# Idle products cut from 512 to 256 columns, and one ones-column memset left out

## The chip, the cores and the metric

The kernel runs on one core of one Trainium2 chip. The metric is the device time of one launch in microseconds (us), taken as the median of several runs. A core has five engines with queues of their own: PE (matrix products; its weight loads are shown as PEld), DVE (vector), ACT (activations), POOL and SP (here a DMA queue only). Each engine takes its instructions in order; they meet through semaphores.

## What is computed

Four batches, eight heads, 768 tokens, head size 64. A small 8 x 8 matrix per head is normalised five times by rows and columns (Sinkhorn) and mixes the eight blocks of 96 tokens of K and of V. Each block of Q attends to the block of the same index. The result, 768 x 512 per batch, goes through a gated MLP with a product over the tokens. Cut to what matters:

```python
for _ in range(5):
    P = np.exp(P - np.max(P, axis=-1, keepdims=True))
    P = P / (np.sum(P, axis=-1, keepdims=True) + 1e-09)
    P = P / (np.sum(P, axis=-2, keepdims=True) + 1e-09)
k_sorted = einsum('bhij,bhjcd->bhicd', P, k_blocks)
v_sorted = einsum('bhij,bhjcd->bhicd', P, v_blocks)
attn = softmax(scale * q_blocks @ k_sorted.T)        # per block
x = (attn @ v_sorted)                                # 4 x 768 x 512
h = np.maximum(x @ w_in, 0.0)                        # 512 -> 1024
u, v = h[..., :512], h[..., 512:]
v_n = (v - mu) / np.sqrt(var + 1e-06)
v_s = einsum('ts,bsd->btd', w_spatial, v_n) + b_spatial[None, :, None]
out = (u * v_s) @ w_out
```

## The kernel before

The order of the work is written out by hand: the string ORDER (L18 to L53) is a list of units such as `AT:0:3:2:0`, each of which calls the function of that name (`u_AT`) with its arguments, and the instructions go to each engine's queue in that order. A unit's first argument is often a PSUM tile: 0 to 3 are pairs of banks, 10 to 17 are single banks, so that tile 0 is banks 10 and 11. The four batches overlap: while batch 1 is in its MLP, attention of batch 2 and 3 is already under way.

The parts that the change touches or that stand around it:

- **Idle products** (`u_DM`, L232 to L235): products of a zeroed tile `warm` with itself into a PSUM tile whose content nobody reads. The arguments are the PSUM tile, the number and the columns of each. 12 stand at the start, ahead of the transposes of Q. Then `DM:12:5:512` and `DM:12:4:512` stand between two groups of transposes of Q (L324), and `DM:10:2:512` stands behind the products that spread P over the partitions (`u_PR`, L265), ahead of V's first mixing products (L393), which need pd. pd is written by DVE (`u_P0`, L279) from the spread P. P comes from DVE's Sinkhorn steps (`u_SK`, L247 to L260).
- **V with its ones column.** For batches 1, 2 and 3, V's mixed blocks are built in the tile `vm` (`u_VM`, L420 to L428), 66 columns per head: 64 of V and two of ones. DMAs from SP's queue copy whole rows, all 66 columns, from `vm` to `vb[b % 2]` (`u_VC`, L433): four DMAs for blocks 0 to 3, four for blocks 4 to 7. The ones column makes the attention product (`u_AT`, L498) give the row sums too, in its 65th column.
- **Three memsets** on POOL write the ones (`u_IV`, L230): `IV:0` into `vb[0]` and `IV:2` into `vm` at the start, and `IV:1` into `vb[1]`, far later: in ORDER it stands in batch 3's attention (L38), behind the issue of V's first four copies of batch 3 (`VC:3:0:4`) and ahead of the second four. Batch 1, which uses `vb[1]` too, ran by then on what the copies had brought.
- **The gate.** For batch 1's four quarters of 128 features (`mc`), the product over tokens (`u_SP`, L619) goes into a PSUM tile, DVE adds the bias (L625) and writes a tile `z`, POOL multiplies z by u (`u_GT`, L636) into `gt`, and the output products (`u_OP`, L645) read gt. There are three z buffers. The gate products of batch 1 stand on POOL directly behind `IV:1`: `GT:P:1:3`, `GT:P:1:1`, `GT:P:1:0`, `GT:P:1:2`. The fourth z (`SP:0:1:2`) takes the buffer that the first gate product frees.
- **What follows it on PE:** `SP:0:1:2`, then scores of batch 3 (`SC:1:3:2:0`, `SC:2:3:2:1`, L452, each with exponentials on ACT, L457), the v half of the MLP's first layer for batch 2 (`VP:16:A:2:5`, L564) and attention of batch 3 (`AT:0:3:2:0`, L498), which writes the same PSUM tile 0 that the addition of `SP:0:1:2` reads.

The last stretch of the order, behind `IF`, runs after a branch on a flag that says that all sums were in range.

Of the kernel before, what the change touches and what calls it, by code (L numbers as in the profile page):

```python
# [16 lines left out]

ORDER = """  # L18
S0 CO DM:10:5:512 IV:0 LH:A:0 TB SK:0 DM:10:3:512 L:q:0:4:8 BH ID SK:1 SK:2 IV:2 QC:A:0 DM:10:4:512 QC:A:1 SK:3 MA
L:v:0:0:8 MC SK:4 QQ:0:A:0:0 DM:12:5:512 DM:12:4:512 L:k:0:0:8 QT:12:D:0:3 PR:13 L:v:1:0:8 MB DM:10:2:512 P0:0:2  # L20
P0:2:4 P0:4:6 P0:6:8 VT:2:A:0:0 PC:A VT:3:D:0:1 QT:12:A:0:2 VB:10:D:0:0 PD:1:0:4 VB:11:A:0:1 VT:2:D:0:3 L:k:1:0:8
VT:3:A:0:2 KT:1:D:0:2 KT:0:A:0:0 KT:2:D:0:1 PD:1:4:8 KT:3:A:0:3 L:q:1:0:8 SC:1:0:2:1 VB:10:D:0:2 VB:11:D:0:3 L:wv L:wu
SC:2:0:3:0 SC:3:0:3:1 L:wsb AT:1:0:2:1 SC:0:0:1:0 L:wsa AT:2:0:3:0 SC:1:0:0:0 AT:3:0:3:1 VM:0:A:1:1 AT:2:0:1:0
# [11 lines left out]
VP:10:D:1:3 SC:1:2:3:0 SC:3:2:1:0 ST:1:0 GT:P:0:1 ST:1:4 QP:A:3:2 ST:1:3 UP:2:A:1:0:1 OP:0:0:2:2 ST:1:5 AT:1:2:2:1  # L35
OE:A:0:2 AT:3:2:3:0 OP:2:0:0:2 LN:1:0:6 LA:1:0 LA:1:5 LA:1:1 QP:A:3:3 OE:A:0:0 OP:0:0:4:2 OE:A:0:4 LA:1:4 LA:1:3
VM:1:A:3:3 VM:3:A:3:1 QP:A:3:0 LA:1:2 SP:2:1:0 XD:2:1 QX:3:0:4 VM:0:A:3:2 AT:1:2:0:0 SP:3:1:1 L:k:3:0:8 VM:2:D:3:0
AT:0:2:1:0 SP:1:1:3 OS:0:2:0:2 UP:3:A:1:1:1 VC:3:0:4 AT:2:2:2:0 KT:0:A:3:0 IV:1 KT:1:D:3:1 XD:2:0 GT:P:1:3 KT:3:D:3:2  # L38
GT:P:1:1 KT:2:A:3:3 SP:0:1:2 SC:1:3:2:0 SC:2:3:2:1 VP:16:A:2:5 AT:0:3:2:0 VP:17:D:2:3 SC:1:3:3:0 SC:2:3:0:1 OS:0:4:0:2
ST:2:3 ST:2:5 SC:0:3:1:1 VP:16:D:2:4 VC:3:4:8:0:4 AT:1:3:3:0 VP:17:A:2:0 UP:2:A:2:1:1 AT:0:3:2:1 VP:16:D:2:2 ST:2:2  # L40
SC:1:3:0:0 ST:2:0 GT:P:1:0 SC:2:3:1:0 SC:0:3:3:1 ST:2:4 VP:17:A:2:1 UP:1:A:2:1:0 ST:2:1 UP:2:A:2:0:0 GT:P:1:2 LN:2:0:6
# [795 lines left out]
```

## Time and profile before

| what | value |
|---|---|
| time, median of 3 runs | 155.23 us (154.25 to 155.38) |
| profiled execution | 155.29 us, of which span 153.5 us |
| busy PE, PEld | 142.8 us (93%), 94.5 us (62%) |
| busy DVE, ACT, POOL | 114.7 us (75%), 85.0 us (55%), 42.5 us (28%) |
| chain that ended last, by engine | PE 77%, DVE 11%, issue 3%, ACT 2%, DMA 2%, POOL 1% |
| memsets of L230 on POOL | 3, of 0.18 to 0.21 us, the last at 91.45 us |
| idle products of L235 | 23 of 512 columns |

The span runs from the first to the last instruction of the core; the time of a run has a little around it. In a row of the timeline, the first two numbers are the start and the duration in us, counted from the span's start; behind the engine and the line stand the operation, the tile that is written and the tiles that are read, and in brackets the idle time of the engine before it, with what ended it. "issue" there means that the engine waited for nothing that the profile shows. In the chain, each row is a piece of the path that ended last. Ends of products on PE are modelled; their starts are recorded.

### The profile page before, as it was taken

How to read it: one execution, taken by the hardware profiler on the slowest of the kernel's cores; microseconds unless marked ns; L12 is line 12 of the kernel's file. 1: busy time of each engine (PE TensorE's matmuls, PEld its weight loads, DVE VectorE, ACT ScalarE, POOL GpSimd, SP SyncE). 2: the span in 40 equal slices, each digit the busy share in tenths (PEclk: the TensorE clock that was granted, in tenths of full speed). 3: DMA queues.
4: the chain of work that ended last, by engine and by line, in shares of the span. 5: the costliest groups of instructions: out<-in, count | busy, mean ns of one | idle time of the engine just before them, and what ended most of it. 6: DMA issues, size and time to landing. Idle time of an engine off the chain costs nothing.

```text
span 153.5 us, 4093 instructions
## 1 busy us (share of the span) xinstructions
PE 142.8 (93%) x1676; PEld 94.5 (62%) x1676; DVE 114.7 (75%) x264; ACT 85.0 (55%) x122; POOL 42.5 (28%) x47
## 2 busy tenths in 40 slices
PE   6578989989999999999999997999999999999791
PEld 2246867854777666855876674558865556855550
DVE  3788889956797882969964965897927989876632
ACT  4464999875889615978976055786230331520040
POOL 7402994290000004832000019500000800005610
PEclk9999999999999999999999999999999999999999
DMA  4999999999999990899993999000093033039046
GB/s 107 253 204 204 189 198 201 208 219 239 233 258 204 204 158 12 146 149 191 205 168 38 293 208 253 9 0 4 0 263 78 4 137 137 2 134 407 22 178 234
DMA packets 30695, 24.38 MB, mean 159 GB/s; under 512 B 10384, under 2 KB 27792, under 8 KB 30672
## 3 DMA queue, kind: packets, MB, share of 16 engines
q0 software_dynamic: 14432, 12.19, 50.1%
q1 hardware_dynamic: 14864, 9.92, 24.6%
q10 hardware_dynamic: 1376, 1.97, 3.7%
q8 instruction: 14, 0.23, 0.6%
q14 instruction: 9, 0.07, 0.1%
HBM read 24.78 MB, written 6.29 MB: 202 GB/s over the span
## 4 chain that ended last, share of the span: by engine, by line
PE 77%; DVE 11%; issue 3%; ACT 2%; DMA 2%; POOL 1%; SPq 1%; ACTq 0%; DVEq 0%; POOLq 0%
PE ps L564 13%; PE ps L607 13%; PE ps L619 13%; PE ps L645 10%; PE ps L675 5%; PE ps L498 5%; PE ps L452 4%; PE ps L695 4%; PE ps L393 3%; PE ps L420 3%; PE ps L528 2%; DMA vb<-vm 2%; PE ps L324 2%; DVE x_sb L506 2%; PE ps L411 1%
## 5 line engine op out<-in xcount | busy, mean ns | idle before, releaser
L636 POOL TENSOR_TENSOR gt<-z,u_sb 128x768 bf16<-128x768 f32 x9 | 14.6, 1637 | 49.6 <-DVE z L625 26.4
L457 ACT ACTIVATE ex_all<-ps 96x768 bf16<-96x768 f32 x32 | 23.9, 805 | 6.0 <-PE ps L452 5.6
L619 PE MATMUL ps<-wspT,v_sb 128*128 128x384 bf16 x144 | 24.9, 326 | 0.0
L564 PE MATMUL ps<-w_in_sb,xT 128*128 128x512 bf16 x96 | 23.4, 380 | 0.0
L607 PE MATMUL ps<-xT,w_in_sb 128*128 128x384 bf16 x128 | 23.1, 326 | 0.0
L506 DVE TENSOR_TENSOR x_sb<-ps,rec_all 96x512 bf16<-96x512 f32 x32 | 22.0, 687 | 1.1
L625 DVE TENSOR_TENSOR z<-ps,b_bc 128x768 f32<-128x768 f32 x12 | 11.4, 954 | 14.2 <-PE ps L619 12.0
L619 PEld LDWEIGHTS <-v_sb 128*128 128x128 bf16 x144 | 13.7, 98 | 8.7
L127 ACT ACTIVATE v_sb<-ps 128x512 bf16<-128x512 f32 (+1 forms) x15 | 9.9, 657 | 15.9 <-DVE bad L722 8.7
L581 DVE BATCH_NORM_STATS2 stats<-v_sb 128x6 f32<-128x512 bf16 x24 | 16.2, 674 | 1.7 <-ACT v_sb L127 1.5
L607 PEld LDWEIGHTS <-w_in_sb 128*128 128x128 bf16 x128 | 12.1, 98 | 7.9
L645 PE MATMUL ps<-w_out_sb,gt 128*128 128x256 bf16 x144 | 16.9, 273 | 0.0
L121 ACT COPY o_sb<-ps 128x1024 f32<-128x1024 f32 (+1 forms) x10 | 8.8, 883 | 13.9 <-PE ps L695 11.4
L127 ACT ACTIVATE u_sb<-ps 128x768 bf16<-128x768 f32 x12 | 9.7, 810 | 10.3 <-PE ps L607 10.3
L645 PEld LDWEIGHTS <-gt 128*128 128x128 bf16 x144 | 13.9, 98 | 2.1
L564 PEld LDWEIGHTS <-xT 128*128 128x128 bf16 x96 | 8.4, 98 | 8.4
L498 PEld LDWEIGHTS <-ex_all 96*128 96x128 bf16 x256 | 10.7, 97 | 4.5 <-issue 1.6
L498 PE MATMUL ps<-vb,ex_all 96*128 96x65 bf16 x256 | 11.8, 193 | 1.0 <-DVE z L625 0.8
L291 POOL TENSOR_TENSOR pd<-mask,prep_sb 128x512 bf16<-128x512 bf16 x6 | 6.6, 1102 | 13.7 <-ACT prep_sb L121 8.9
L688 POOL TENSOR_TENSOR gt<-z,u_sb 128x512 bf16<-128x512 f32 (+1 forms) x5 | 5.2, 1048 | 18.4 <-DVE z L681 18.4
L121 ACT CAST vm<-ps 128x768 bf16<-128x768 f32 x9 | 7.2, 808 | 4.9 <-PE ps L420 4.7
L452 PE MATMUL ps<-qT,kt_all 64*128 64x96 bf16 x256 | 8.8, 204 | 0.8 <-issue 0.4
(100 smaller groups left out, 205.5 us busy)
## 6 DMA issues: line engine op xcount, KB each, us to landing
out_dram<-o_sb SPq DMA_DIRECT2D x8, 512.0 KB, 3.5
v_in<-in_v_dram POOLq DMA_DIRECT2D x4, 768.0 KB, 13.3
k_in<-in_k_dram POOLq DMA_DIRECT2D x4, 768.0 KB, 10.9
vb<-vm SPq DMA_DIRECT2D x24, 99.0 KB, 3.6
q_in<-in_q_dram POOLq DMA_DIRECT2D x3, 768.0 KB, 25.4
ws_in<-in_moe_w_spatial_dram POOLq DMA_DIRECT2D x2, 576.0 KB, 18.9
w_in_sb<-in_moe_w_in_dram POOLq DMA_DIRECT2D x2, 512.0 KB, 13.2
q<-in_q_dram ACTq DMA_DIRECT2D x1, 768.0 KB, 4.5
```

What stands on the lines that cost most here:

```text
L121: nc.scalar.copy(out=out, in_=in_)
L127: nc.scalar.activation(out=out, in_=in_, func=AF.Relu)
L452: nc.tensor.matmul(t[:, hh, 0:HW].rearrange("p (g x) -> p g x", g=G)[:, :, ii * TB:(ii + 1) * TB], lhsT=kT[rows, i * BLK:i * BLK + 128], r ...
L457: nc.scalar.activation(out=e_tile(b, hp, ih).rearrange("p h (x g) -> p h x g", g=G), in_=t[0:BLK, :, 0:HW].rearrange("p h (g x) -> p h x g ...
L498: nc.tensor.matmul(t[:, hh, ii * VW:ii * VW + D + 1], lhsT=e[:, c:c + 128], rhs=vb[b % 2][:, ih * NI + ii, 2 * hp + hh, 0:D + 1], start=Tr ...
L506: nc.vector.tensor_mul(out=x_sb[:, hp].rearrange("p i (h d) -> p h i d", h=2), in0=tv[:, :, :, 0:D], in1=_raw_ap(rec, 0, [rec.ap[0], [NI, ...
L564: nc.tensor.matmul(t[:, x, :], lhsT=st["xT", b][:, n // 3, kc, (n % 3) * 128:(n % 3 + 1) * 128], rhs=w_in_sb[:, kc, DH:DFF], start=(kc == ...
L581: nc.vector.bn_stats(out=stats, in_=st["v_sb", b, n])
L607: nc.tensor.matmul(t[:, x, 0:HW], lhsT=w_in_sb[:, kc, mc * 128:(mc + 1) * 128], rhs=st["xT", b][:, ih, kc, :], start=(kc == 0), stop=(kc = ...
L619: nc.tensor.matmul(t[:, x, 0:HW], lhsT=st["v_sb", b, n][:, mc * 128:(mc + 1) * 128], rhs=wspT[:, 3 * x:3 * x + 3, n, :], start=(n == 0), s ...
L636: eng.tensor_mul(out=gt, in0=st["z", b, mc], in1=u)
L645: nc.tensor.matmul(t[:, x, c:c + w], lhsT=st["gt", b, mc][:, (n0 + x) * 128:(n0 + x + 1) * 128], rhs=w_out_sb[:, mc, c:c + w], start=(mc = ...
```

## The change

The 11 later idle products of 512 columns become 22 of 256, so that the columns are the same in number. The 12 at the start stay. The memset of the ones columns of `vb[1]` is taken out of the order; the functions stay as they are.

```diff
-L:v:0:0:8 MC SK:4 QQ:0:A:0:0 DM:12:5:512 DM:12:4:512 L:k:0:0:8 QT:12:D:0:3 PR:13 L:v:1:0:8 MB DM:10:2:512 P0:0:2
+L:v:0:0:8 MC SK:4 QQ:0:A:0:0 DM:12:10:256 DM:12:8:256 L:k:0:0:8 QT:12:D:0:3 PR:13 L:v:1:0:8 MB DM:10:4:256 P0:0:2
...
-AT:0:2:1:0 SP:1:1:3 OS:0:2:0:2 UP:3:A:1:1:1 VC:3:0:4 AT:2:2:2:0 KT:0:A:3:0 IV:1 KT:1:D:3:1 XD:2:0 GT:P:1:3 KT:3:D:3:2
+AT:0:2:1:0 SP:1:1:3 OS:0:2:0:2 UP:3:A:1:1:1 VC:3:0:4 AT:2:2:2:0 KT:0:A:3:0 KT:1:D:3:1 XD:2:0 GT:P:1:3 KT:3:D:3:2
```

On the engines' queues: PE has 11 weight loads and 11 products more, in two places (9 pairs become 18, and 2 pairs become 4). POOL has one memset less, with its wait for five DMA semaphores. SP's second four V copies no longer wait for POOL. DVE's and ACT's queues are the same. Each idle product loads its weights anew, before as after.

## The prediction

> **What bounds the kernel now.** I read the page first, then the table of six stretches, then the chain of waits between 82 and 95 us, then PE's list of waits, and last the timeline around both edits.
>
> ```profile
> span 153.5 us, 4093 instructions
> ```
> ```profile
> 85.00:94.30 9.30, 8.47 (x109) 5.41 (x108) 6.58 (x10) 4.24 (x6) 2.85 (x3) 1.00 1.07 273
> 94.30:144.00 49.70, 49.70 (x413) 32.07 (x412) 39.56 (x88) 17.09 (x27) 10.74 (x8) 1.00 0.30 98
> ```
> The columns of the second fence are the stretch, its length, then the busy time of PE, PEld, DVE, ACT and POOL, the granted clock, the DMA share and the GB/s. From 94.30 to 144.00 PE is busy 49.70 of 49.70 us, at a granted clock of 1.00. So a start of PE at 94.3 that comes earlier by x brings the end earlier by x, unless something off PE falls behind. In the stretch before it PE loses 9.30 - 8.47 = 0.83 us, and the waits and the chain say to whom:
>
> ```profile
> PE ps L498 <- DVE z L625: 0.8, 1, 0.8
> ```
> ```profile
> 91.45 0.20 POOL L230 MEMSET vb<- 96x128 bf16 x1 [21.34 <-DMA vb<-vm]
> ```
> ```profile
> 91.45 0.13 POOL vb L230
> 91.58 0.04 issue
> 91.62 1.64 POOL gt L636
> 93.28 0.97 DVE z L625
> 94.25 0.04 issue
> 94.29 0.40 PE ps L498 x8
> ```
> The first fence is PE's list of waits, the second the timeline, the third the chain. The memset that goes is a link of the chain. It waits on POOL for V's first four copies of batch 3, which had therefore landed by about 91.4, it holds back the gate product queued behind it, that product holds a z buffer, the addition that writes z waits for the buffer, and attention (L498) waits for the addition, since both use the same PSUM banks.
>
> **The change part by part. The memset.** It ran 0.20 us, but what counts is when the gate product (L636) could start without it. Its inputs are the z addition at 87.09 and the ReLU that writes u at 88.24:
>
> ```profile
> 75.77 3.49 PE ps L645 x32
> ```
> ```profile
> 87.09 0.94 DVE L625 TENSOR_TENSOR z<-ps,b_bc 128x768 f32<-128x768 f32 x1
> 88.24 0.81 ACT L127 ACTIVATE u_sb<-ps 128x768 bf16<-128x768 f32 x1 [5.09 <-PE ps L607]
> 89.92 2.12 PE L619 MATMUL ps<-wspT,v_sb 128*128 128x384 bf16 x12
> 92.36 1.50 ACT L457 ACTIVATE ex_all<-ps 96x768 bf16<-96x768 f32 x2 [1.54 <-PE ps L452]
> 92.42 1.04 PE L564 MATMUL ps<-w_in_sb,xT 128*128 128x512 bf16 x4
> ...
> 96.11 1.04 PE L564 MATMUL ps<-w_in_sb,xT 128*128 128x512 bf16 x4
> 96.98 0.41 PE L498 MATMUL ps<-vb,ex_all 96*128 96x65 bf16 x8
> ```
> They are ready at 88.03 and 89.05, and the output products that read the last batch's gate tiles ended at 79.26 (first row, of the chain). So the product starts at about 89.1 in place of 91.62 and, at its 1.64 us, ends at about 90.8. The z addition is then no longer held by POOL but by its matmuls, which end at 89.92 + 2.12 = 92.04. Two earlier pairs give the gap between such an end and the addition:
>
> ```profile
> 79.75 2.11 PE L619 MATMUL ps<-wspT,v_sb 128*128 128x384 bf16 x12
> 82.00 0.96 DVE L625 TENSOR_TENSOR z<-ps,b_bc 128x768 f32<-128x768 f32 x1 [2.67 <-PE ps L619]
> 93.22 0.10 PEld L498 LDWEIGHTS <-ex_all 96*128 96x128 bf16 x1 [0.26 <-ACT ex_all L457]
> ```
> 82.00 - 81.86 = 0.14, and the pair at 82.27 and 84.52 gives the same to 0.01. The addition runs from 92.18 to 93.14, and frees PE at 93.18 (the chain shows 0.04 between them). Two other things must be there: the exponentials, of which the first ends at 92.36 + 0.75 = 93.11, with the weight load at 93.22; and PE itself, which starts attention 0.87 after such a group of four (96.11 to 96.98), so at 92.42 + 0.87 = 93.29. The last of the three is PE's own work: the wait is gone altogether, and attention starts at 93.29 in place of 94.29. That is 1.00 us. If PE is counted busy until the modelled end of the group, 93.46, it is 0.83. I take 1.00, because the start-to-start distance is measured and the end is modelled. The next to be late are the exponentials, by 0.07 us, and the addition, by 0.11.
>
> What else hung on the memset: SP's second four V copies waited for it, but SP was issuing an output until 90.95 + 0.75 = 91.70, and the copies start at 91.82, so they gain 0.1 at most. They also have to keep up: attention's second half at 99.39 moves to 98.39.
>
> ```profile
> 90.95 0.75 SPq L660 DMA_DIRECT2D out_dram<-o_sb  x1
> 91.82 2.61 SPq L433 DMA_DIRECT2D vb<-vm  x4
> DMA to landing us min/median/max: 2.8/3.0/3.3
> 99.39 0.41 PE L498 MATMUL ps<-vb,ex_all 96*128 96x65 bf16 x8
> ```
> The last of the four is issued before 94.43 and lands by 94.43 + 3.3 = 97.7, so 0.7 us is left. The first attention of batch 3 reads copies that landed by 91.4, 1.9 us before 93.29. POOL's other three gate products move with the first and their readers (L645 at 104.9) are far. The ones column itself costs nothing: the copies carry all 66 columns.
>
> **The idle products.** 9 of the 11 lie between two groups of transposes, 2 behind the products that spread P.
>
> ```profile
> 8.33 2.12 PE L235 MATMUL ps<-warm 128*128 128x512 bf16 x9
> 10.38 0.53 PE L324 MATMUL ps<-ident,q_in 128*64 128x128 bf16 x12
> 11.69 0.35 PE L265 MATMUL ps<-p_t,spread 32*128 32x32 bf16 x8 [0.78 <-DVE p_t L260]
> 11.96 0.60 PE L235 MATMUL ps<-warm 128*128 128x512 bf16 x2
> 12.74 0.47 PE L393 MATMUL ps<-pd,v_in 128*64 128x128 bf16 x10 [0.17 <-DVE pd L279]
> 105.09 1.75 PE ps L645 x16
> L645 PE MATMUL ps<-w_out_sb,gt 128*128 128x256 bf16 x144 | 16.9, 273 | 0.0
> L645 PEld LDWEIGHTS <-gt 128*128 128x128 bf16 x144 | 13.9, 98 | 2.1
> ```
> The nearest row for 256 columns with a weight load each is L645: 1.75 / 16 = 0.109 us. Eighteen take 1.97 us, against 10.38 - 8.33 = 2.05 now; four take 0.44 against about 0.46. Behind the first group PE waits 0.78 us for DVE's Sinkhorn steps, behind the second 0.17 us for pd. So the term is 0, and it stays 0 up to (2.05 + 0.78) / 18 = 0.157 us a product. Without that cover each 0.1 us on a product would cost 1.8 us. The other end is 0.273 us, the mean duration of one such product, if none overlapped the next: 18 x 0.273 - 2.05 - 0.78 = 2.08, and 4 x 0.273 - 0.46 - 0.17 = 0.46, together 2.5 us late. I take 0.109, as L645 has the same shapes and pattern.
>
> [...]
>
> PE also gets 22 instructions more (11 loads, 11 products). There is one bare stall in the crowded part, with no wait behind it:
>
> ```profile
> 31.94 0.54 PE L452 MATMUL ps<-qT,kt_all 64*128 64x96 bf16 x17 [0.43 <-issue]
> q8 instruction: 14, 0.23, 0.6%
> ```
> Fourteen packets of 0.23 MB are 16.4 KB each, for 2 x 1676 PE records: about 240 a packet. If the stall is a late packet, it moves 22 instructions forward, and may vanish (-0.43) or come twice (+0.43); I take 0, since nothing shows which. [...]
>
> **The sum.** 0 for the products, -1.00 for the memset, 0 for the fetch. The profiled execution took 155.29 us for its span of 153.5; it stands 0.06 above the median of the runs, 155.23. 155.29 - 1.00 = 154.3 us, 0.6% less.
>
> **The rivals.** *Weights do not overlap.* Each pair then takes 0.098 + 0.109 = 0.207 us: 18 x 0.207 - 2.05 - 0.78 = 0.90 late, and 4 x 0.207 - 0.63 = 0.20, so 155.29 - 1.00 + 1.10 = 155.4, no change. L645 speaks against it; for it, only that the idle products take their weights and columns from one tile. [...]
>
> *Products queue up, slower than before.* All write the same PSUM columns; if each waited for the end of the one before, 2.5 us would be added: 155.29 - 1.00 + 2.5 = 156.8. It outweighs the gain from about 0.20 us a product. Against it: the 512-column ones do so too and go every 2.05 / 9 = 0.23 us.
>
> *The earlier gate product blocks DVE.* It would now run beside DVE's casts of K:
>
> ```profile
> 89.33 1.81 DVE L123 CAST kt_all<-ps 128x768 bf16<-128x768 f32 x2
> 16.45 1.11 POOL L291 TENSOR_TENSOR pd<-mask,prep_sb 128x512 bf16<-128x512 bf16 x1
> 16.71 1.81 DVE L123 CAST kt_all<-ps 128x768 bf16<-128x768 f32 x2
> ```
> Casts pushed from 89.33 behind 90.8 would end at 92.6 instead of 91.14, and the scores at 91.97 would come 0.6 later: 154.9. Against it: beside POOL at 16.71 the two casts took the same 1.81 us. [...]
>
> *The fetch stall goes or doubles:* 153.9 or 154.7. *The memset matters to nobody:* the trace cannot show what else the gate product would have waited for while the memset stood ahead of it. If something else holds it to 91.6, nothing is gained: 155.3; each 0.1 us of its start past 90.5 (92.18 - 1.64) takes 0.1 from the gain. Against it: both inputs and its buffer are there by 89.05, on the rows above.
>
> **How the numbers follow.** Forecast 0.63; fetch stall gone 0.13, doubled 0.06; DVE blocked 0.04; no overlap 0.04; queueing 0.03; memset without effect 0.07. The three runs of before lie between 154.25 and 155.38, so each case carries some 0.5 us of scatter. From 153.5 to 155.4 holds the forecast, both fetch cases and the blocked case nearly whole and half of the two that end at the old time. A change of 1%, 1.55 us, is about the least that a measurement of this kernel tells from none. Faster by more, below 153.7, takes the stall gone or the scatter's low end: 0.63 x 0.13 + 0.13 x 0.45 + a little = 0.15. Slower by more takes the queueing: 0.04 with scatter. The rest, 0.81, is within 1%.
>
> **What would show it.** PE's wait of L498 for z is gone and the first gate product starts near 89.1; the z addition starts 0.14 after L619 and not at a POOL end; L235 shows 18 products in 1.97 us and the 0.78 us wait behind them is still there; the span is 152.5. I am wrong if the products of 256 columns go slower than 0.157 us, if PE shows idle time between 93.3 and 143, or if a bare stall near 31 us changes by more than 0.43.

## The result, and the profile after

The changed kernel takes 153.38 us (median of 6 runs, 153.07 to 154.13), the kernel before 155.31 (median of 6, 154.25 to 156.26). The ratio is 0.9889, with a 95% interval from 0.9843 to 0.9936: 1.1% faster, some 1.7 us. The forecast was 154.3, with a range from 153.5 to 155.4. By the ratio the result is 0.9889 x 155.29 = 153.6 us, just inside that range. The direction was right, the gain too small by almost half: what was missing came from a place that the prediction had not priced. The interval of the gain, 1.0 to 2.4 us, only just reaches the forecast of 1.0; which part of the change gave what is shown by the experiments below.

First the table of stretches of the kernel after (columns as before: stretch, length, busy PE, PEld, DVE, ACT and POOL, clock, DMA share, GB/s):

```profile
85.00:94.30 9.30, 9.30 (x128) 6.20 (x127) 7.06 (x10) 3.55 (x5) 4.47 (x3) 1.00 1.02 263
94.30:144.00 49.70, 49.70 (x412) 32.06 (x408) 39.86 (x89) 17.78 (x28) 8.95 (x7) 1.00 0.31 100
```

The 0.83 us that PE had lost between 85.0 and 94.3 are gone, and the rest of the stretch is as full as it was. The timeline of the kernel after shows how:

```profile
88.93 0.81 ACT L127 ACTIVATE u_sb<-ps 128x768 bf16<-128x768 f32 x1 [5.10 <-PE ps L607]
89.83 6.44 POOL L636 TENSOR_TENSOR gt<-z,u_sb 128x768 bf16<-128x768 f32 x4 [19.04 <-ACT u_sb L127]
90.61 2.12 PE L619 MATMUL ps<-wspT,v_sb 128*128 128x384 bf16 x12
92.87 0.96 DVE L625 TENSOR_TENSOR z<-ps,b_bc 128x768 f32<-128x768 f32 x1 [1.04 <-PE ps L619]
93.11 1.04 PE L564 MATMUL ps<-w_in_sb,xT 128*128 128x512 bf16 x4
93.99 0.41 PE L498 MATMUL ps<-vb,ex_all 96*128 96x65 bf16 x8
```

The gate products now start 0.09 us after u's ReLU. The z addition names PE as its releaser, no longer POOL, and starts 90.61 + 2.12 + 0.14. Attention starts 0.88 us after the group of four, with no wait. All of it stands 0.7 us later than forecast (the addition at 92.87 and not at 92.18, attention at 93.99 and not at 93.29), for a reason that lies ahead of both edits: in this execution the first load, that of the 8 x 8 matrices, landed later, 2.54 us behind its issue against 1.6 in the kernel before, as the chain of the kernel after shows.

```profile
0.74 2.54 DMA p_all<-in_sort_net_dram
3.31 0.26 ACT p_all L247
```

In the execution of before, the first exponential of P started at 2.59. The products that spread P (L265) start at 11.67 to 11.69 there and in all twelve experiments, and at 12.40 in this execution. So the two spans (153.5 and 152.3) understate the gain by 0.72 us: 1.2 + 0.72 = 1.9 us.

Where the other 0.9 us went is seen at the end. PE's list of waits of the kernel before had this row, third from the top, which the prediction did not use, and the timeline of before shows the place:

```profile
PE ps L695 <- issue: 0.8, 1, 0.8
```
```profile
144.86 5.37 PE L695 MATMUL ps<-w_out_sb,gt 128*128 128x512 bf16 x32 [0.84 <-issue]
```

The same row of the kernel after has no idle time in front of it:

```profile
143.56 5.36 PE L695 MATMUL ps<-w_out_sb,gt 128*128 128x512 bf16 x32
```

L695 is the first work behind the branch (`IF` in the order). Before, PE stood there for 0.84 us without waiting for anything that the profile shows; after, it does not. The bare stall near 31 us is still there, 0.45 us, and has moved from the scores to the transposes (L528). That is 22 instructions earlier in the program, and so at the same place in the count of PE's instructions:

```profile
32.23 0.33 PE L528 MATMUL ps<-ident,x_sb 96*128 96x96 bf16 x4 [0.45 <-issue]
```

And the idle products themselves cost what was expected of them:

```profile
9.04 2.14 PE L235 MATMUL ps<-warm 128*128 128x256 bf16 x18
11.11 0.53 PE L324 MATMUL ps<-ident,q_in 128*64 128x128 bf16 x12
12.40 0.35 PE L265 MATMUL ps<-p_t,spread 32*128 32x32 bf16 x8 [0.76 <-DVE p_t L260]
```

Eighteen pairs of load and product took 11.11 - 9.04 = 2.07 us, 0.115 us each, against 2.05 us for the nine of 512 columns, and the wait behind them was 0.76 us, against 0.78.

### The profile page after: what moved, and what is told of

Read it like the earlier page. It is cut to its first block, busy times and chain, and to the rows that moved or that the text cites. A ratio compares the mean times of both kernels' runs of the same rounds, so it can differ in the third digit from the quotient of the medians.

```text
span 152.3 us, 4112 instructions
## 1 busy us (share of the span) xinstructions
PE 143.7 (94%) x1687; PEld 95.9 (63%) x1687; DVE 114.7 (75%) x264; ACT 85.0 (56%) x122; POOL 42.3 (28%) x46
## 4 chain that ended last, share of the span: by engine, by line
PE 83%; DVE 10%; DMA 2%; issue 1%; ACT 1%; DVEq 0%
PE ps L619 15%; PE ps L564 14%; PE ps L607 14%; PE ps L645 10%; PE ps L675 5%; PE ps L498 5%; PE ps L452 4%; PE ps L393 4%; PE ps L695 3%; PE ps L420 3%; PE ps L528 2%; PE ps L324 2%; DVE x_sb L506 2%; DMA p_all<-in_sort_net_dram 2%; PE ps L411 1%
## 5 line engine op out<-in xcount | busy, mean ns | idle before, releaser
L498 PEld LDWEIGHTS <-ex_all 96*128 96x128 bf16 x256 | 10.7, 97 | 3.6 <-issue 0.6
L498 PE MATMUL ps<-vb,ex_all 96*128 96x65 bf16 x256 | 11.8, 193 | 0.2 <-DVE x_sb L506 0.2
L235 PE MATMUL ps<-warm 128*128 128x256 bf16 (+1 forms) x34 | 8.1, 400 | 1.3 <-DVE warm L209 1.3
## 6 DMA issues: line engine op xcount, KB each, us to landing
w_in_sb<-in_moe_w_in_dram POOLq DMA_DIRECT2D x2, 512.0 KB, 12.4
```

The lines of the kernel that those rows point to most:

```text
L498: nc.tensor.matmul(t[:, hh, ii * VW:ii * VW + D + 1], lhsT=e[:, c:c + 128], rhs=vb[b % 2][:, ih * NI + ii, 2 * hp + hh, 0:D + 1], start=Tr ...
```

## The experiments

Two questions: which part of the change gave what, and why the stall ahead of L695 went. The products and the memset touch different things, so each was tried alone first. Times are medians; the kernel before was run beside them on the same chip.

| run | edit against before | PE instructions more | stall ahead of L695, us | time, us | ratio to before (95%) |
|---|---|---|---|---|---|
| e1 | memset out | 0 | 0.82 | 153.75 | 0.9933 (0.9911 to 0.9955) |
| e2 | 22 of 256 | 22 | none | 154.11 | 0.9954 (0.9936 to 0.9972) |
| e3 | memset out, 11 of 256 | 0 | 0.84 | 154.78 | 0.9984 (0.9963 to 1.0005) |
| e4 | memset out, 22 of 128 | 22 | none | 153.82 | 0.9935 (0.9907 to 0.9963) |
| e5 | memset out, 15 of 256 | 8 | 0.90 | 153.93 | 0.9974 (0.9951 to 0.9998) |
| e6 | memset out, 5 of 256 | -12 | 0.78 | 155.21 | 1.0040 (1.0022 to 1.0058) |
| e7 | memset moved up | 0 | 0.88 | 153.70 | 0.9936 (0.9913 to 0.9959) |
| e8 | memset out, 30 of 128 | 38 | none | 153.61 | 0.9928 (0.9908 to 0.9947) |
| e9 | memset out, 1 of 256 | -20 | 0.80 | 155.33 | 1.0041 (1.0017 to 1.0066) |
| e10 | memset out, 19 of 256 | 16 | none | 153.03 | 0.9886 (0.9848 to 0.9924) |
| e11 | 11 of 128 more, early | 22 | none | 154.11 | 0.9949 (0.9932 to 0.9967) |
| e12 | e11, memset out | 22 | none | 153.21 | 0.9902 (0.9873 to 0.9931) |

In the expectations below, a refill is the author's name for the coming of a packet on the instruction queue; that PE waits for one is the theory under test.

**e1: the memset alone.**

```diff
-AT:2:2:2:0 KT:0:A:3:0 IV:1 KT:1:D:3:1
+AT:2:2:2:0 KT:0:A:3:0 KT:1:D:3:1
```

> Only the memset is out; the eleven products of 512 columns are as before. Both theories take the wait of attention (L498) for z away, which is worth 0.8 to 1.0 us. Theory A (the stall of 0.84 us ahead of L695 is late instructions behind the branch, and it goes because PE has 22 instructions more between two refills and the branch): the stall stays, time about 154.3. Rival B (the stall went because POOL has one instruction less or gets to the branch earlier): the stall is gone here too, time about 153.4.

The ratio gives (1 - 0.9933) x 154.9 = 1.04 us, with an interval from 0.70 to 1.38; the prediction had 1.00. L498 no longer waits, and the stall ahead of L695 stays, as the rows of e1's timeline show:

```profile
91.90 0.96 DVE L625 TENSOR_TENSOR z<-ps,b_bc 128x768 f32<-128x768 f32 x1 [1.04 <-PE ps L619]
93.02 0.41 PE L498 MATMUL ps<-vb,ex_all 96*128 96x65 bf16 x8
143.57 5.37 PE L695 MATMUL ps<-w_out_sb,gt 128*128 128x512 bf16 x32 [0.82 <-issue]
```

So rival B, that POOL's shorter queue takes the stall away, falls.

**e2: the products alone.** The diff is that of the change without the line of `IV:1`.

> Only the products are cut, the memset stays where it was. Theory A: the stall ahead of L695 is gone, the wait of L498 for z of 0.8 us is there as before; time about 155.3 - 0.9 = 154.4. Rival B: the stall stays and nothing is gained, 155.3. Rival C (the stall comes and goes from one execution to the next): either, and no difference of the medians.

The ratio gives 0.71 us (0.43 to 0.99). The wait for z is there, the stall is not:

```profile
93.94 0.40 PE L498 MATMUL ps<-vb,ex_all 96*128 96x65 bf16 x8 [0.62 <-DVE z L625]
143.51 5.36 PE L695 MATMUL ps<-w_out_sb,gt 128*128 128x512 bf16 x32
```

1.04 + 0.71 = 1.75 us, and the whole change gave (1 - 0.9889) x 155.31 = 1.72. Within these intervals the two parts add.

**e7: the memset kept, but ahead of the copies.**

```diff
-VC:3:0:4 AT:2:2:2:0 KT:0:A:3:0 IV:1 KT:1:D:3:1
+IV:1 VC:3:0:4 AT:2:2:2:0 KT:0:A:3:0 KT:1:D:3:1
```

> The products are as before; the memset stays, but ahead of V's first four copies of batch 3, so that it waits for none of them. If its place behind the copies was what cost the time, the wait of L498 for z is gone and the time is that of the memset left out: about 154.3, with the stall of 0.84 us ahead of L695. If the memset itself costs on POOL or DVE, it stays near 155.3.

0.99 us gained with the memset still in the program. In POOL's timeline it runs long before it matters, and the gate products start right behind u:

```profile
69.56 0.24 POOL L230 MEMSET vb<- 96x128 bf16 x1
88.60 6.45 POOL L636 TENSOR_TENSOR gt<-z,u_sb 128x768 bf16<-128x768 f32 x4 [18.80 <-ACT u_sb L127]
```

What cost the time was not the memset's 0.2 us but its place: a wait for DMAs on POOL's queue, ahead of the gate products.

**e3 and e4: columns or instructions.** Both have 11 x 256 = 22 x 128 idle columns, half of the change's. From here to e10 the diffs are against the changed kernel, so the memset is out.

```diff
-DM:12:10:256 DM:12:8:256
+DM:12:5:256 DM:12:4:256
...
-DM:10:4:256
+DM:10:2:256
```

> The memset is out, the eleven products have 256 columns each, so the idle columns are halved and the number of PE's instructions is that of the kernel before. Theory A: the number of instructions counts, so the stall of 0.84 us ahead of L695 is back and the bare stall near 31 us stands in the scores (L452) as before; time about 154.3. Rival D (shorter products are what helps): the stall is gone, 153.4 or less.

```diff
-DM:12:10:256 DM:12:8:256
+DM:12:10:128 DM:12:8:128
...
-DM:10:4:256
+DM:10:4:128
```

> The memset is out, 22 products of 128 columns: the number of instructions is that of the changed kernel, the idle columns are half. Theory A: no stall ahead of L695 and the bare stall near 31 us in the transposes (L528), as in the changed kernel; time about 153.4. Rival D (columns of idle work count, by the clock or otherwise): the stall ahead of L695 returns, or TensorE slows down, about 154.3 or more.

With the number of instructions of before the stall is back (0.84 us); with that of the change it is gone, at the same idle columns. But e3 was slower than expected by 0.5 us, and e4 by 0.4, and that is a cost of its own: the granted clock, the share of its full speed that PE was given. In e3's table of stretches, the third number from the end is the clock:

```profile
12.00:13.00 1.00, 0.62 (x10) 0.44 (x11) 0.89 (x5) 0.00 (x0) 0.00 (x0) 0.71 1.31 204
13.00:14.00 1.00, 1.00 (x24) 1.00 (x22) 0.67 (x3) 0.39 (x1) 0.00 (x0) 0.50 1.31 204
14.00:15.00 1.00, 1.00 (x20) 0.83 (x16) 0.74 (x1) 0.79 (x3) 0.23 (x1) 0.50 1.31 201
15.00:16.00 1.00, 1.00 (x13) 1.00 (x12) 0.28 (x2) 0.69 (x1) 1.00 (x2) 0.58 1.31 204
```

The clock falls to one half from about 12.4 to 15.8 us, in the middle of the first products for K and V. This happened in 10 of e3's 12 executions (mean clock 0.986 to 0.989, 154.4 to 155.1 us; the two others 153.5 and 153.9) and in 4 of e4's 9 (154.2 to 154.5 against 153.0 to 153.8). So the idle columns are not without a use: with half of them left, the clock fell in 14 of these 21 executions.

**e5 and e6: is the stall graded by the number?**

```diff
-DM:12:10:256 DM:12:8:256
+DM:12:5:256 DM:12:6:256
...
 DM:10:4:256
```

> The memset is out, 15 products of 256 columns: four pairs more than the kernel before. Theory A: the refill is asked for four products (4 x 0.109 us) earlier ahead of the branch, so the stall ahead of L695 is about 0.84 - 0.44 = 0.4 us; time about 153.9. If only the crossing of some fixed point counts, it is 0.84 or 0.

```diff
-DM:12:10:256 DM:12:8:256
+DM:12:3:256
...
-DM:10:4:256
+DM:10:2:256
```

> The memset is out, five products of 256 columns: six pairs fewer than the kernel before. Theory A: the refill comes six products later, and the stall ahead of L695 grows to about 0.84 + 0.65 = 1.5 us; time about 155. Rival D (less idle work costs nothing or helps): no longer stall than 0.84, 154.3.

No: 0.90 us with 8 instructions more, 0.78 with 12 fewer. The theory of a packet that simply starts earlier by as many products as are added falls. e5 lost the clock in 5 of 12 executions (154.7 to 155.1 against 153.8 to 153.9, so some 1.1 us), e6 in all 12 (mean clock 0.978 to 0.989). That is most of why e6 is slower than before although the memset is out.

**e8: more of them.**

```diff
-DM:12:10:256 DM:12:8:256
+DM:12:14:128 DM:12:12:128
...
-DM:10:4:256
+DM:10:4:128
```

> The memset is out, 30 products of 128 columns, 26 of them in the first place: eight pairs more than the changed kernel. Theory A: no stall ahead of L695, as in the changed kernel; the bare stall near 31 us moves 16 instructions further back and may change by some tenths. The idle products take 26 x 0.1 = 2.6 us and stay inside the 2.8 us that PE has there. Time about 153.4; more than 0.3 us below would come from the bare stall alone.

No stall, 153.61. The clock stayed up (0.997 to 1.000 in all six).

**e9 and e10: a step, and where.** A second form of the theory was that PE's queue stops at waits, so that the moment at which the packet starts moves in steps.

```diff
-DM:12:10:256 DM:12:8:256
+DM:12:1:256
...
-DM:10:4:256
```

> The memset is out, one idle product of 256 columns is left of the eleven: PE has 20 instructions fewer than before. Theory A2 (the refill ahead of the branch is asked for when PE's queue passes a fixed instruction number; the queue stands at waits in between, so that the moment moves in steps with the wait that lies ahead of that number): the number now lies one wait later (the products of L675 that wait for the fourth z), and the stall ahead of L695 grows in one step to 1.7 to 2.3 us. Graded theory A: 0.84 + 10 x 0.109 = 1.9, but the runs with 5 and 15 products speak against it. Rival E (the branch costs either 0.8 to 0.9 or nothing): 0.8 to 0.9. The clock falls near 12 us as with five products; the time is about 155.2 plus what the stall grows.

```diff
-DM:12:10:256 DM:12:8:256
+DM:12:10:256 DM:12:5:256
```

> The memset is out, 19 products of 256 columns: 16 instructions more than before, between the 8 that kept the stall and the 22 that took it away. Theory A2: the step is where the fixed number passes the wait 12 instructions ahead of it, so the stall is gone, as with 22; time about 153.4 where the clock stays up. Graded theory A: 0.84 - 8 x 0.109, so nearly gone too. Rival F (22 more is the step, by where the code behind the branch lies): stall of 0.9, about 154.

e9 has 0.80 us, so the second form falls too, as it was put: nothing grew. (Its time of 155.33 has the clock in it, which fell in all ten executions, to a mean of 0.976 to 0.985.) e10 has no stall and 153.03 us, a little below the change's figure but inside its interval. The stall is 0.78 to 0.90 us or nothing, and the step lies between 8 and 16 instructions more:

```profile
144.73 5.37 PE L695 MATMUL ps<-w_out_sb,gt 128*128 128x512 bf16 x32 [0.80 <-issue]
```
```profile
142.35 5.36 PE L695 MATMUL ps<-w_out_sb,gt 128*128 128x512 bf16 x32
```

(The first row is e9's timeline, the second e10's.)

**e11 and e12: the instructions in another place.** The diff is against the kernel before. The eleven of 512 stay as they were; eleven more of 128 columns stand where PE waits for Q.

```diff
-DM:10:4:512 QC:A:1
+DM:10:4:512 DM:10:11:128 QC:A:1
```

> The kernel before with its eleven products of 512 columns and its memset; eleven more idle products of 128 columns stand in the gap of PE ahead of the first transposes, where PE waits for Q. PE has the 22 instructions more, but the late idle products are untouched. Theory A2: the stall ahead of L695 is gone and the wait of L498 for z stays; the time is that of the products alone, about 154.1. If the form of the late products counts, nothing changes: 154.8.

> As the run with eleven more early products, and the memset out. Theory A2: both gains, with the clock up for certain: 153.0 to 153.4, the changed kernel's time. If the two gains were not independent: above 153.8.

e11 gained 0.79 us, as much as e2 within the intervals, and its timeline has the wait for z and no stall:

```profile
93.96 0.40 PE L498 MATMUL ps<-vb,ex_all 96*128 96x65 bf16 x8 [0.65 <-DVE z L625]
143.53 5.36 PE L695 MATMUL ps<-w_out_sb,gt 128*128 128x512 bf16 x32
```

With the memset out as well, e12 reached 153.21. So the form of the late products did not matter for the stall, only how many instructions PE has ahead of the branch: with 22 more there was none in e2, e4, e11 and e12 alike. No run beat the change clearly: e10, e12 and the change lie within each other's intervals.

**What ended ahead of PE's restart: the instruction packets.** The DMA records of the same executions show what came in ahead of the branch. The prediction counted 14 packets of 16.4 KB on the instruction queue q8. The thirteenth lies just ahead of L695, and narrow windows of the DMA view give its start and its duration. The first row is the kernel before from 142.37 to 142.40, the second the kernel after from 141.06 to 141.09; the last number is the packet's time as a share of 16 engines in the window:

```profile
q8 instruction: 1, 0.02, 221.7%
```
```profile
q8 instruction: 1, 0.02, 200.2%
```

2.217 x 0.03 x 16 = 1.06 us, so the packet of before ended at 143.44, and L695's first weight load started at 144.85, 1.41 us later. That of the kernel after took 0.96 us and ended at 142.03, 1.45 us before L695's first load at 143.48. All fourteen kernels together, counted from the first product of L675, the last group ahead of the branch:

| PE instructions more | kernels | packet's start, us behind L675's first product | L695's first load, us behind the packet's end | stall ahead of L695, us |
|---|---|---|---|---|
| -20, -12, 0, 8 | 7 | 6.16 to 6.46 | 1.40 to 1.44 | 0.78 to 0.90 |
| 16, 22 | 6 | 5.11 to 5.31 | 1.43 to 1.62 | none |
| 38 | 1 | 0.25 ahead of it | 6.93 | none |

Wherever PE stood ahead of L695, it went on 1.40 to 1.44 us behind the end of this packet. With 16 or 22 instructions more the packet started about 1 us earlier, and L675's products, of which the last starts 7.69 us behind the first, covered it just in time. The bare stall near 31 us follows the same queue: in the five executions that have it (before, after, e1, e2, e11) PE goes on 1.46 to 1.55 us behind the end of the third packet, each time at the same place in the order of PE's recorded instructions, to within one. That PE stood for late instructions at both places is the author's reading of these times, from one profiled execution of each kernel.

## Why the prediction was right and where it was wrong

*The memset: right, by its steps.* Forecast 1.00 us, measured 1.04 (0.70 to 1.38) in e1 and 0.99 (0.63 to 1.35) in e7. The product starts behind u's ReLU, the addition behind its matmuls at 0.14, attention 0.88 behind the group of four, where 0.87 was forecast. The copies behind it kept up. The profile of before held all of it: the chain named the links, and each link's other input had a row.

*The idle products' own time: right.* 0.115 us a pair against 0.109, and the cover of 0.78 us was hardly touched (0.76 after). The rivals *Weights do not overlap*, which needed 0.207 us a pair, and *Products queue up*, priced at 0.273, fall with this row. The term was 0 with the columns kept the same in number; what they do for the clock the prediction did not consider, and e3 to e6 and e9 show what fewer of them cost: with 256 to 3840 columns left of 5632, the clock fell in 5 of 12 executions (e5) to all (e6, e9), for some 1.1 us in e5. In e8 (3840) and e10 (4864) it fell in none.

*The earlier gate product blocks DVE: no.* DVE's two casts of K beside it took what they took before:

```profile
90.02 1.81 DVE L123 CAST kt_all<-ps 128x768 bf16<-128x768 f32 x2
```

*The fetch: the step that failed.* The prediction gave the 22 instructions the term 0, with 0.43 us to both sides, because it took the stall near 31 us for the only one that could move. That one did move by the 22 instructions, but its size changes from one execution to the next: 0.43 us before, 0.17 in e1's and none in e7's list of waits, though all three have PE's program of before. The stall whose presence depended on the number was the one ahead of L695, 0.84 us. It stood in the list of waits, under "issue", and the prediction does not mention it; its signs of being wrong, a stall near 31 us and idle time between 93.3 and 143, could not show it either. The kind of cause that the times point to, a late packet, was named, and put at the wrong place: the case of the stall gone (153.9, chance 0.13) priced the other one. The term should have been about -0.8 (0.71 measured in e2, 0.79 in e11) instead of 0, and the sum 155.29 - 1.00 - 0.84 = 153.45, next to the measured 153.38.

*What stays open.* Why the packet ahead of the branch starts about 1 us earlier from 16 instructions more on, and neither earlier nor later between -20 and 8, no run tells; nor what the 1.4 us between its end and PE's next instruction are. No trace here shows which code the packet held.

## What to carry to other kernels

A short instruction that waits for a transfer is priced by what is queued behind it on its engine, not by its own duration (0.20 us here): follow that work's other inputs, and the gain comes out within what the runs can tell (1.00 forecast, 1.04 and 0.99 measured, each to some 0.35 us). A stall that the profile puts down to "issue" need not be a constant (0.78 to 0.90 us in seven kernels here, none in seven): look in the DMA records for an instruction packet that ends ahead of it (by 1.40 to 1.44 us here), and when an edit changes the number of instructions before it, give it its full size as one end of the range. Idle products are read by what they hold up: look at the granted clock before shortening them (0.50 for about 3.4 us in e3's profiled execution).

## What was not expected of the hardware

- A stall of 0.78 to 0.90 us behind a branch came and went with the number of PE's instructions ahead of it: present at -20, -12, 0 and 8 more, absent at 16, 22 and 38. Where it was present it ended 1.40 to 1.44 us behind the end of an instruction packet.
- The granted clock fell to 0.50 with PE far from idle: in e3 PE was busy 1.26 of the 3 us between 9 and 12, where it had been 2.22 in the kernel before, and its longest single wait was 1.74 us.

```profile
9.00:12.00 3.00, 1.26 (x26) 0.94 (x24) 2.70 (x12) 1.57 (x2) 0.00 (x0) 1.00 1.32 204
```
```profile
9.00:12.00 3.00, 2.22 (x28) 1.22 (x27) 2.70 (x12) 1.57 (x2) 0.00 (x0) 1.00 1.31 203
```

(The first row is e3's, the second that of the kernel before.) From the four rows of e3 above, the clock was down for 0.29 / 0.5 + 1 + 1 + 0.42 / 0.5 = 3.4 us, an estimate that takes it to have stood at 1.00 or at 0.50. PE was busy for over a third of the 3 us ahead of the fall. What keeps the clock no run tells: e4, with the same columns in twice as many products, kept it in five of nine executions, with PE busy 1.29 of the same 3 us in one of them; e5 and e8 have 3840 columns each, and e5 lost it in 5 of 12 executions, e8 in none of 6.
